# Decay rows of one half batch moved into matmuls of their own, and the first value loads moved forward in the load queue

## The chip, the cores and the metric

The kernel runs on one core of a Trainium2 chip. The metric is the device time of one execution in microseconds; 272.35 us is the median of five executions before the change (271.96 to 273.83). A separate execution was recorded by the profiler: it took 271.63 us, of which 269.7 us lie between its first and its last instruction (the span). All times inside the kernel are counted from the start of that span.

Engine names: PE is the matrix engine (PEld its weight loads), DVE the vector engine, ACT or ScalarE the activation engine, POOL the general engine, SP the engine that here only issues DMA transfers. SPq, ACTq and POOLq are their DMA-issuing queues.

## The reference

Eight batches of eight heads, 576 positions, head width 64, then a feed-forward block with a 3-tap convolution:

```python
scores = (q @ k.T) / sqrt(64) + cum[i] - cum[j]     # cum = cumsum(log(clip(f)))
attn   = softmax(where(j > i, -1e9, scores))
x      = (attn @ v), heads side by side              # 576 x 512 per batch
h      = relu(x @ w_in)                              # 576 x 1024
gate   = sigmoid(conv3(h, conv_w))                   # along the positions
out    = (h * gate) @ w_out                          # 576 x 512
```

All inputs and the output are fp32. The term `cum[i] - cum[j]` is called the decay.

## The kernel before, in words

**Tiling.** Work on attention is cut into 16 half batches `hb` of four heads, and each of these into two head pairs `i`. Scores are held transposed, keys on the partitions and queries along the row. For a pair there is one block of diagonal tiles (`diag_scores`, L326, eight 128x128 matmuls onto a causal mask that a matmul by the identity, L330, puts down first), and per head one block of the tiles off the diagonal (`off_scores`, L315, matmuls of 448, 64, 320 and 192 columns); the last 64 keys of all four heads form one tail block (`tail_scores`, L301). ScalarE takes each block to an fp16 tile by one exp (L338, L324, L310). `pv` (L340) multiplies these by the values `va`, whose 65th column is one, so that the softmax sum comes along; `norm` (L359) divides.

**Queries and keys.** `load_qk` (L106) loads q and k by transposing DMAs on SP. An fp32 number is transposed as two 16-bit halves, so of 128 partitions the odd ones hold the upper halves, which are used as bf16, and the even ones hold lower halves. `clamp` (L116) multiplies the even partitions by zero on DVE. Three even partitions then carry the decay: k's 96 and 98 hold the upper and lower bf16 part of minus `cum` over the scale, against ones in q; q's 126 holds the upper part against minus one in k. So a single matmul of full height gives q·k plus decay. There is a ring of four q tiles (`stq`) and four k tiles (`stk`).

Who puts the decay rows in differs. For half batch 0 `clamp` writes the constants, and ScalarE (first pair) and POOL (second pair) issue small row DMAs (`rows_first`, L122). For half batch 1, `clamp` stops at partition 96, POOL copies constant rows from the tile `consts` (`fill`, L129) and then three rows from `khi_sb` and `klo_sb` (`rows_of`, L139 to L143). From half batch 2 on the rows come by way of DRAM (`kd`). `fill_sources` (L542) writes `consts` by three memsets on DVE, early. From half batch `CLAMPS` (8) on, q's even partitions are cleared by a constant copy of 48 rows on POOL in place of DVE's clamp.

**Values.** `load_v` (L158) loads fp32 values by SP, five DMAs a half batch, into two buffers `vf`, one per batch in turn; `cast_v` (L167) brings them to fp16 on DVE. The first load is held until a one-element memset of DVE (L250), so that it is not issued ahead of that point. `HALVES` (16) says up to which half batch values are loaded by halves.

**MoE.** After both half batches of a batch, its attention output is transposed on PE (`xpose_pe`) and copied (`xpose_out`). Per 128 columns of d_ff: `moe1` (L420) on PE, `relu` (L430) on ScalarE into one of four `ht` tiles, two `conv` steps on DVE (L455, L457), `tanh` on ScalarE, `gate` (L469) on DVE, which frees the `ht` tile; `moe2` (L484) then multiplies by w_out, 128 positions at a time.

**What sets the order.** Instructions up to L269 stand in the order written. From L527 on the kernel keeps a list of tasks, each with the engines it may run on, an assumed duration, what it depends on, a key (a due time in units of head pairs) and the buffers that it takes and gives. `play` (L713) plays this list through before anything is built and hands out, engine by engine, the ready task with the lowest key; the result is a fixed order of instructions per engine. Each engine runs its own list strictly in order. `hold` (L149) is a one-element write that keeps a later weight load from being issued early; `WAITS` (L550) names the half batch and the side whose preparation releases each of the four loads of w_out.

**Queues.** SP issues one transfer after another. In the program as built a transfer issued by SP or ScalarE also waits for the end of the transfer issued eight before it on these two; POOL's have the same rule among themselves. SP's order before is: q and k of half batch 0 (four transfers), q1, k1, ten loads of batch 0's values, q2, k2, five loads of values, q3, k3, and so on.

Of the kernel before, what the change touches and what calls it, by code (L numbers as in the profile page):

```python
# [9 lines left out]
FP32 = mybir.dt.float32  # L10
# [8 lines left out]
def kernel(  # L19
# [11 lines left out]
    nc = tc.nc  # L31
# [103 lines left out]
    def rows_of(hb):  # L135

        tq, tk = stq_t[hb % RING], stk_t[hb % RING]
        c = slice(hb * HH, (hb + 1) * HH)
        if hb == 1:  # L139
            nc.gpsimd.dma_start(tk[96:97, 0:HS], khi_sb[c, :])  # L140
            nc.gpsimd.dma_start(tk[98:99, 0:HS], klo_sb[c, :])
            nc.gpsimd.dma_start(tq[126:127, 0:HS], khi_sb[c, :])
            return  # L143
        nc.gpsimd.dma_start(tq[126:127, 0:HS], kd[0:1, c, :].rearrange("j h s -> j (h s)"))
        row = HS + 64
        nc.gpsimd.dma_start(bass.AP(tensor=tk.tensor, offset=int(tk.offset) + 96 * row, ap=[[2 * row, 2], [1, HS]]),
                            kd[:, c, :].rearrange("j h s -> j (h s)"))

# [86 lines left out]
    load_qk(1, 0, 4)  # L235
    for side in range(2):
        clamp(0, side, 0, 2)
    rows_first(0, nc.scalar)

# [10 lines left out]
    nc.vector.memset(vf_t[0][0:1, 0, 0, 0:1], 0.0)  # L250
    load_v(0, 0, HH)
    load_v(0, HH, H)
# [14 lines left out]
    for t in range(NHT):  # L267
        nc.gpsimd.memset(ht_t[t][:, :, 0:HT_0], 0.0)
        nc.gpsimd.memset(ht_t[t][:, :, HT_0 + S:HT_W], 0.0)  # L269

# [25 lines left out]
    def scores(sc, hb, k0, q0, w, start=True, stop=True):  # L296

        nc.tensor.matmul(sc, stk_t[hb % RING][:, k0:k0 + 128], stq_t[hb % RING][:, q0:q0 + w],  # L298
                         start=start, stop=stop, skip_group_check=True)
# [242 lines left out]
    def fill_sources():  # L542
        z = consts.bitcast(FP32)
        nc.vector.memset(z, 0.0)
        nc.vector.memset(z[0:2, :], PAIR)
        nc.vector.memset(z[32:33, :], MINUS)

    CLAMPS, HALVES, LANDING = 8, 16, 3.0
    HELD, POOLED = 4, 4
    WAITS = ((3, 0), (3, 1), (4, 0), (4, 1))  # L550
# [8 lines left out]
    t_fsrc = task({"DVE": 3.1}, [], -9, fill_sources)  # L559
    for hb in range(NHB):  # L560
        key = 2 * hb - 5.5
        ring = [x for j in range(2) for x in t_qk[hb - RING, j]] if hb >= RING else []
        b = hb // 2
        even, landed = [], []
        for s in range(2):
            if hb == 1:
                x = task({"ACT": 0.01}, [], -9, lambda: None, lag=(0.3, 3.8)[s])
            elif hb:
                last = x = task({"SP": 3.0}, ring, key + 0.1 * s, lambda hb=hb, s=s: load_qk(hb, 0, 4, s),
                                lag=LANDING, dma=3.1, behind=last)  # L570
            if hb:
                landed.append(x)
            if hb:
# [5 lines left out]
            if hb and (s or hb < CLAMPS):  # L579
                even.append(task({"DVE": 0.9}, [x], (2 * hb - 3 if hb > 1 else -5) + 0.2 * s,  # L580
                                 lambda hb=hb, s=s: clamp(hb, s, 0, 4, 96)))
        t_half = None
        if b == 0 and hb < 2:
            t_half = task({"ACT": 0.01}, [], -9, lambda: None, lag=(6.5, 9.3)[hb])
            t_v[b] = t_half
        elif hb < HALVES:
            last = t_half = task({"SP": 3.2}, [t_cast[hb - 4, p] for p in range(2)] if b >= 2 else [], key + 0.2,
                                 lambda b=b, h=HH * (hb % 2): load_v(b, h, h + HH), lag=2.3, dma=3.0, behind=last)
        elif hb % 2 == 0:
            last = t_v[b] = task({"SP": 3.5}, [t_cast[2 * b - j, p] for j in (4, 3) for p in range(2)] if b >= 2 else [],  # L590
                                 key + 1.2, lambda b=b: load_v(b), lag=2.3, dma=6.0, behind=last)
# [4 lines left out]
        if hb:  # L596
            t_rows[hb] = even + [task({"POOL": 1.1 if hb > 1 else 1.6}, landed, 2 * hb - 3.6 if hb > 1 else -9 if hb > 1 else -1.0,
                                      lambda hb=hb: rows_of(hb), lag=LANDING + 1.0)]
        else:
            t_rows[hb] = []  # L600
        for p in range(2):
            t_cast[hb, p] = task({"DVE": 0.75 if p == 0 else 0.42},
                                 [t_half or t_v[b]] + ([t_pv[2 * hb - 5, 1]] if hb >= 3 else []), 2 * hb - 1.1 + 0.5 * p,
                                 lambda hb=hb, p=p: cast_v(hb, p, nc.vector), lag=0.2)

        for p in range(2):
# [10 lines left out]
            x = task({"PE": 0.9}, t_rows[hb], i + 0.1, lambda i=i: diag_scores(i), take="sc")  # L617
            t_qk[hb, p] = [t_tail, x]
            mask = task({"ACT": 1.02}, [x], i + 0.1, lambda i=i: diag_exp(i), take="pm", give=[("sc", x)])
            for s in range(2):  # L620
                x = task({"PE": 0.46}, t_rows[hb], i + 0.2 + 0.4 * s, lambda i=i, s=s: off_scores(i, s),
# [9 lines left out]
            t_norm[i] = task({"DVE": 1.05}, [t_pv[i, 1]], i - 0.0, lambda i=i: norm(i) if i else [norm(i), hold(w_in_f16)],  # L631
                             take="xn" if i % PPB == 0 else None, give=[("O", t_pv[i, 0])])
            if i == 0:
                t_win = task({"POOL": 1.0}, [t_norm[0]], -0.5, lambda: nc.gpsimd.dma_start(
                    w_in_f16, moe_w_in.rearrange("(cc p) ff -> p cc ff", p=128)), lag=2.0, dma=6.5)
        if hb % 2:
# [10 lines left out]
    start = [PPB * (b0 + nb) + 1.0 for b0, nb in GROUPS]  # L647
    start += [start[-1] + 4.0, start[-1] + 6.0]
    t_exp, t_late = [], []
    for g, (b0, nb) in enumerate(GROUPS):  # L650
# [3 lines left out]
        for ff in range(NFF):  # L654
            key = start[g] + 0.8 * (start[g + 1] - start[g]) * ff / NFF
            relus = []
            for t in range(nt):
# [5 lines left out]
                relus.append(task({"ACT": 0.18 + w / 1200.0}, [x] + relus[0:1], key + 0.05 * t - 1.5,  # L663
# [10 lines left out]
            t_gate[g, ff] = task({"DVE": 0.1 + n / 1800.0 if g == LAST else 0.2 + n / 1050.0}, [x], key - 1.5, lambda g=g, ff=ff: gate(g, ff),  # L674
# [36 lines left out]
    AHEAD, QUEUED = 3.0, 8.0  # L711

    def play():  # L713
        busy = {"PE": 11.5, "ACT": 12.0, "DVE": 12.0, "POOL": 14.0, "SP": 19.0}
        ready = {e: [] for e in busy}
        dma_free, clock = 21.5, 0.0
# [112 lines left out]
```

## Time and profile before

| | |
|---|---|
| median of five executions | 272.35 us (271.96 to 273.83) |
| profiled execution, its span | 271.63 us, 269.7 us |
| busy over the span: PE, DVE, ACT, POOL | 241.1, 226.5, 211.8, 58.9 us |
| mean granted PE clock | 0.981 |
| PE idle of 0 to 80 us; of 80 to 230 us | 20.0 us; 0.7 us |
| first score matmul of half batch 0, of half batch 1 | 11.4, 24.5 us |
| first moe1 matmul, first conv | 37.36, 40.02 us |
| transfers on SP's queue | 32.0 MB, 69.1% of 16 DMA engines' span |

Busy time is a sum over one engine's instructions; 89% for PE is a mean over a beginning in which it waits and a long stretch in which it never does. In rows of stretches the columns are: stretch, its length, busy us and count for each engine, granted PE clock (1.00 is full speed), mean busy share of the DMA engines, GB/s. In rows of the timeline: start, duration, engine, line, operation, output and input, count, and in brackets how long the engine had been idle and what ended that. In rows of waits: who waited for whom, us in total, how often, the longest.

### The profile page before, as it was taken

The numbers are of one execution on the slowest core, as the hardware profiler recorded it, in microseconds if no ns is written. First come the engines' busy times: TensorE is split into PE (matmuls) and PEld (weight loads), VectorE is DVE, ScalarE is ACT, GpSimd is POOL, SyncE is SP. The second block draws the span as 40 slices with busy tenths as digits, with TensorE's granted clock in tenths as the row PEclk, the third lists the DMA queues.
The fourth block names the chain that finished last, engine by engine and source line by source line (L and its number), as shares of the span: only waits on it lengthen the run. The fifth ranks groups of instructions, "written<-read, shape, count | busy, mean of one in ns | idle before, by whom it ended". The sixth has DMA issues, their size and how long they took to land.

```text
span 269.7 us, 6621 instructions
## 1 busy us (share of the span) xinstructions
PE 241.1 (89%) x2602; PEld 165.1 (61%) x2602; DVE 226.5 (84%) x401; ACT 211.8 (79%) x347; POOL 58.9 (22%) x124
## 2 busy tenths in 40 slices
PE   2955779877999999999999999999999999989990
PEld 1334557655777677676776677667776767554640
DVE  5963539999799999999989989999899999978751
ACT  5171829889879999989988898989999998577552
POOL 4491110631221240332415050404110100000000
PEclk9997979999999999999999999999999999999997
DMA  7999999999999999999999999999410201022015
GB/s 140 224 195 185 220 179 211 192 233 195 199 204 200 210 244 187 220 223 239 258 200 178 216 268 192 190 119 252 128 48 32 80 0 71 10 117 80 0 48 226
DMA packets 121284, 44.58 MB, mean 165 GB/s; under 512 B 115560, under 2 KB 116596, under 8 KB 121254
## 3 DMA queue, kind: packets, MB, share of 16 engines
q1 hardware_dynamic: 115088, 32.00, 69.1%
q0 software_dynamic: 5840, 12.01, 16.7%
q8 instruction: 20, 0.33, 0.5%
q10 hardware_dynamic: 326, 0.17, 0.3%
q14 instruction: 10, 0.08, 0.1%
HBM read 13.99 MB, written 9.58 MB: 87 GB/s over the span
## 4 chain that ended last, share of the span: by engine, by line
PE 62%; DMA 9%; DVE 7%; SPq 7%; issue 6%; ACT 6%; POOL 0%; ACTq 0%; DVEq 0%; POOLq 0%
PE mm L425 18%; PE mm L487 18%; PE sc L298 10%; PE O L356 7%; DMA stk<-in_k_dram 6%; SPq L110 5%; PE sc L330 4%; DMA vf<-in_v_dram 2%; PE sc L500 2%; SPq L163 2%; DVE u L457 2%; DVE u L455 2%; PE mm L393 2%; ACT ht L438 1%; DMA out_dram<-ob 1%
## 5 line engine op out<-in xcount | busy, mean ns | idle before, releaser
L425 PE MATMUL mm<-xt,w_in_f 128*128 128x288 f16 x512 | 79.9, 290 | 1.7 <-DVE xt L413 0.4
L298 PE MATMUL sc<-stq,stk 128*128 128x128 bf16 (+3 forms) x576 | 67.1, 242 | 7.4 <-ACT pm L338 3.6
L324 ACT ACTIVATE po<-sc 128x1024 f16<-128x1024 f32 x64 | 64.5, 1028 | 2.0 <-PE sc L298 1.5
L438 ACT ACTIVATE ht<-mm 128x288 f16<-128x288 f32 x128 | 52.0, 414 | 11.7 <-PE mm L425 10.7
L298 PEld LDWEIGHTS <-stk 128*128 128x128 bf16 x576 | 42.4, 99 | 28.4 <-issue 8.5
L425 PEld LDWEIGHTS <-w_in_f 128*128 128x128 f16 x512 | 47.7, 99 | 18.6 <-issue 3.4
L487 PE MATMUL mm<-w_out_f,hg 128*128 128x512 f16 x248 | 58.4, 379 | 0.7 <-ACT xt L411 0.6
L455 DVE SCALAR_TENSOR_TENSOR u<-ht,cwt 128x576 f32<-128x576 f16 x64 | 51.5, 812 | 5.4 <-ACT ht L438 4.7
L457 DVE SCALAR_TENSOR_TENSOR u<-ht,cwt,u 128x576 f32<-128x576 f16 x64 | 51.5, 811 | 0.5
L475 DVE SCALAR_TENSOR_TENSOR hg<-hg,ht 128x576 f16<-128x576 f16 x56 | 41.7, 752 | 3.8 <-ACT hg L467 3.5
L467 ACT ACTIVATE hg<-u,cwt 128x576 f16<-128x576 f32 x56 | 43.4, 779 | 1.0 <-DVE u L457 0.9
L338 ACT ACTIVATE pm<-sc 128x1024 f16<-128x1024 f32 x32 | 32.9, 1027 | 12.0 <-PE sc L298 11.9
L487 PEld LDWEIGHTS <-hg 128*128 128x128 f16 x248 | 23.5, 98 | 24.3 <-issue 0.9
L356 PE MATMUL O<-va,po 128*128 128x65 f16 x640 | 36.5, 194 | 1.2 <-ACT po L324 1.0
L356 PE MATMUL O<-va,pm 128*128 128x65 f16 x256 | 31.1, 194 | 3.0 <-DVE xn L369 1.8
L356 PEld LDWEIGHTS <-po 128*128 128x128 f16 x640 | 30.5, 97 | 2.4 <-ACT po L324 1.8
L132 POOL DMA_DIRECT2D stq<-consts x23 | 12.6, 549 | 75.3 <-PE sc L298 34.2
L356 PEld LDWEIGHTS <-pm 128*128 128x128 f16 x256 | 24.1, 98 | 5.7 <-DVE xn L369 2.7
L369 DVE TENSOR_TENSOR xn<-O,rc 128x640 f16<-128x640 f32 x32 | 26.4, 825 | 1.1
L330 PE MATMUL sc<-trib,identb 128*128 128x512 bf16 x64 | 24.7, 387 | 1.5 <-ACT po L324 1.4
L511 ACT ACTIVATE ob<-mm 128x512 f32<-128x512 f32 x23 | 13.7, 597 | 11.1 <-PE mm L487 10.7
L522 POOL DMA_DIRECT2D out_dram<-ob x10 | 7.5, 748 | 40.1 <-ACT ob L511 20.7
(112 smaller groups left out, 222.5 us busy)
## 6 DMA issues: line engine op xcount, KB each, us to landing
vf<-in_v_dram SPq DMA_DIRECT2D x64, 128.0 KB, 3.9
out_dram<-ob POOLq DMA_DIRECT2D x10, 512.0 KB, 5.2
out_dram<-ob SPq DMA_DIRECT2D x10, 256.0 KB, 2.1
stq<-consts POOLq DMA_DIRECT2D x8, 216.0 KB, 4.6
vf<-in_v_dram SPq DMA_DIRECT2D x16, 64.0 KB, 5.2
w_in_f<-in_moe_w_in_dram POOLq DMA_DIRECT2D x1, 1024.0 KB, 10.4
w_out_f<-in_moe_w_out_dram POOLq DMA_DIRECT2D x4, 256.0 KB, 5.7
out_dram<-ob SPq DMA_DIRECT2D x2, 512.0 KB, 2.8
```

Of the source, the lines that this page charges most:

```text
L298: nc.tensor.matmul(sc, stk_t[hb % RING][:, k0:k0 + 128], stq_t[hb % RING][:, q0:q0 + w], start=start, stop=stop, skip_group_check=True)
L324: nc.scalar.activation(p_of[i, s][:, 0:1024], sc_of.pop((i, s)), AF.Exp, scale=SCALE)
L330: nc.tensor.matmul(sc[:, 512 * s:512 * (s + 1)], identb, trib, start=True, stop=False, skip_group_check=True)
L338: nc.scalar.activation(p_of[i, 2], sc_of.pop((i, 2)), AF.Exp, scale=SCALE)
L356: nc.tensor.matmul(O[:, s, 65 * Q:65 * (Q + 1)], w, va[:, h, m, :], start=(m == 0), stop=(m == Q))
L425: nc.tensor.matmul(ps[:, 0:w], w_in_f16[:, cc, 128 * ff:128 * (ff + 1)], xt[:, cc, w * t:w * (t + 1)], start=(cc == 0), stop=(cc == NCC - 1))
L438: nc.scalar.activation(ht[:, 0, HT_0 + w * t:HT_0 + w * (t + 1)], ps[:, 0:w], AF.Relu)
L455: nc.vector.scalar_tensor_tensor(u, hl, cwt[:, ff, 0:1], hc, op0=ALU.mult, op1=ALU.add)
L457: nc.vector.scalar_tensor_tensor(u, hr, cwt[:, ff, 1:2], u, op0=ALU.mult, op1=ALU.add)
L467: nc.scalar.activation(hv, u, AF.Tanh, scale=cwt[:, ff, 2:3])
L475: nc.vector.scalar_tensor_tensor(hv, hv, 1.0, hc, op0=ALU.add, op1=ALU.mult)
L487: nc.tensor.matmul(ps, chunk(g, ff, c), w_out_f16[:, ff, :], start=(ff == 0), stop=(ff == NFF - 1))
```

## The change

The diff does eight things, in the order of the program.

1. SP's order at the start: q1, first half of batch 0's values, k1, second half of the values. What holds the first values is no longer a memset on DVE but a one-element activation on ScalarE, behind its issue of the first pair's decay rows.
2. ScalarE writes two tiles, `dk` and `dq`, inside the values buffer of batch 1 (`vf_t[1]`, not yet in use): `dk` is zero but for minus ones in its first three rows, `dq` is one everywhere. POOL then copies the upper and lower parts of half batch 1's decay into `dk`'s rows 0 and 1 and the upper part into `dq`'s row 2 (`load_decay`), right after the rows of half batch 0's second pair.
3. For half batch 1 each score matmul is followed by a second one, `dk` by `dq`, onto the same output: 36 more matmuls. Its q and k are clamped over all 128 partitions, and its constant fills and its `rows_of` go.
4. The loads of batch 1's values wait for the scores of half batch 1, since they overwrite `dk` and `dq`.
5. `consts` is written after the norm of pair 1, as three tasks.
6. `warm`: two matmuls of 512 columns into an unused buffer, five times, with the lowest urgency, after the second pair of half batch 0.
7. `CLAMPS` 8 to 6, `HALVES` 16 to 8, `WAITS` later for the first load of w_out.
8. Keys and assumed costs of the planner: norm, clamp, cast, relu, gate, the start of each MoE group, and how many us of transfers may be queued.

```diff
-        if hb == 1:
-            nc.gpsimd.dma_start(tk[96:97, 0:HS], khi_sb[c, :])
-            nc.gpsimd.dma_start(tk[98:99, 0:HS], klo_sb[c, :])
-            nc.gpsimd.dma_start(tq[126:127, 0:HS], khi_sb[c, :])
-            return
...
+    def decay_tiles(hb, dk, dq):
+        dec_of[hb] = dk, dq
+        for t, x in ((dk, 0.0), (dk[0:3], MINUS), (dq, PAIR)):
+            z = t.bitcast(FP32)
+            nc.scalar.activation(z, one1[0:z.shape[0]].broadcast_to(z.shape), AF.Copy, bias=x, scale=0.0)
+
+    def load_decay(hb):
+        (dk, dq), c = dec_of[hb], slice(HH * hb, HH * (hb + 1))
+        nc.gpsimd.dma_start(dk[0:1, 0:HS], khi_sb[c, :])
+        nc.gpsimd.dma_start(dk[1:2, 0:HS], klo_sb[c, :])
+        nc.gpsimd.dma_start(dq[2:3, 0:HS], khi_sb[c, :])
...
-    load_qk(1, 0, 4)
+    load_qk(1, 0, 4, 0)
     for side in range(2):
         clamp(0, side, 0, 2)
     rows_first(0, nc.scalar)
+    nc.scalar.mul(vf_t[0][0:1, 0, 0, 0:1], one1[0:1, 0:1], 0.0)
+    load_v(0, 0, HH)
+    load_qk(1, 0, 4, 1)
+    load_v(0, HH, H)
+    early = vf_t[1].rearrange("p h k d -> p (h k d)")
+    decay_tiles(1, early[:, 0:HS // 2 + 32].bitcast(BF16), early[:, HS // 2 + 32:HS + 32].bitcast(BF16))
...
     rows_first(1, nc.gpsimd)
-    nc.vector.memset(vf_t[0][0:1, 0, 0, 0:1], 0.0)
-    load_v(0, 0, HH)
-    load_v(0, HH, H)
+    load_decay(1)
...
+    def warm():
+        ps = mm_pool.tile([128, 512], FP32, name="mm")
+        for t in range(2):
+            nc.tensor.matmul(ps, identb, trib, start=True, stop=True)
...
-                         start=start, stop=stop, skip_group_check=True)
+                         start=start, stop=stop and hb not in dec_of, skip_group_check=True)
+        if hb in dec_of:
+            dk, dq = dec_of[hb]
+            nc.tensor.matmul(sc, dk[:, k0:k0 + 128], dq[:, q0:q0 + w],
+                             start=False, stop=stop, skip_group_check=True)
...
-    CLAMPS, HALVES, LANDING = 8, 16, 3.0
+    CLAMPS, HALVES, LANDING = 6, 8, 3.0
-    WAITS = ((3, 0), (3, 1), (4, 0), (4, 1))
+    WAITS = ((3, 1), (3, 1), (4, 0), (4, 1))
+    WARM = {0: 5}
...
-    t_fsrc = task({"DVE": 3.1}, [], -9, fill_sources)
+        if hb == 2:
+            t_fsrc = None
+            for z in ((0, 96, 0.0), (0, 2, PAIR), (32, 33, MINUS)):
+                t_fsrc = task({"DVE": 1.03}, [t_norm[1], t_fsrc], 3.0, lambda z=z: fill_source(*z))
...
-            last = t_half = task({"SP": 3.2}, [t_cast[hb - 4, p] for p in range(2)] if b >= 2 else [], key + 0.2,
+            last = t_half = task({"SP": 3.2}, [t_cast[hb - 4, p] for p in range(2)] if b >= 2 else
+                                 t_qk[1, 0] + t_qk[1, 1], key + 0.2,
...
-            t_norm[i] = task({"DVE": 1.05}, [t_pv[i, 1]], i - 0.0, lambda i=i: norm(i) if i else [norm(i), hold(w_in_f16)],
+            t_norm[i] = task({"DVE": 1.05}, [t_pv[i, 1]], i - 0.5, lambda i=i: norm(i) if i else [norm(i), hold(w_in_f16)],
...
+        if hb in WARM:
+            x = None
+            for _ in range(WARM[hb]):
+                x = task({"PE": 0.44}, [t_pv[2 * hb + 1, 1], x], 999, warm, take="mm", lag=0.05)
...
-    start = [PPB * (b0 + nb) + 1.0 for b0, nb in GROUPS]
-    start += [start[-1] + 4.0, start[-1] + 6.0]
+    start = [PPB * (b0 + nb) + x for (b0, nb), x in zip(GROUPS, (1.0, 1.0, 1.5, 2.0, 1.5, 1.0, 1.0, 1.0))]
+    start += [PPB * B + 5.0, PPB * B + 7.0]
...
-                relus.append(task({"ACT": 0.18 + w / 1200.0}, [x] + relus[0:1], key + 0.05 * t - 1.5,
+                relus.append(task({"ACT": 0.18 + w / 1200.0}, [x] + relus[0:1], key + 0.05 * t - 2.0,
...
-            t_gate[g, ff] = task({"DVE": 0.1 + n / 1800.0 if g == LAST else 0.2 + n / 1050.0}, [x], key - 1.5, ...
+            t_gate[g, ff] = task({"DVE": 0.1 + n / 1800.0 if g == LAST else 0.2 + n / 1050.0}, [x], key - 0.0, ...
...
-    AHEAD, QUEUED = 3.0, 8.0
+    AHEAD, QUEUED = 3.0, 10.0
```

## The prediction

> **What bounds the kernel now.** I read the busy times of stretches first, since a share over the whole span mixes stages. The columns are the stretch, PE, PEld, DVE, ACT and POOL busy (with counts), granted PE clock, DMA share, GB/s:
>
> ```profile
> 20.00:25.00 5.00, 1.74 (x36) 1.46 (x37) 1.79 (x6) 0.09 (x1) 0.84 (x2) 0.87 1.20 169
> 25.00:30.00 5.00, 4.68 (x42) 3.29 (x41) 1.54 (x3) 3.35 (x5) 1.01 (x2) 0.79 1.16 216
> 35.00:40.00 5.00, 3.26 (x20) 2.08 (x21) 1.56 (x4) 1.83 (x3) 0.97 (x2) 0.74 1.23 166
> 45.00:50.00 5.00, 4.66 (x67) 3.52 (x64) 4.97 (x10) 5.00 (x9) 2.17 (x3) 1.00 1.33 172
> 65.00:70.00 5.00, 3.96 (x58) 2.95 (x55) 4.97 (x8) 4.16 (x6) 1.31 (x2) 1.00 1.16 217
> 100.00:120.00 20.00, 19.98 (x228) 14.37 (x226) 18.84 (x31) 18.29 (x34) 3.52 (x8) 1.00 1.18 217
> ```
>
> Three regimes: until 40 us nobody is full (everything waits for arrivals), from 45 to 70 DVE is (4.97 of 5), from 80 PE is (19.98 of 20). So a microsecond is won or lost in two ways only: by when the first MoE block hands DVE its long queue of work (40.02), and by PE work or PE gaps after about 70. What holds the first MoE block back is read from the timeline and the waits of 20 to 35 us:
>
> ```profile
> 12.57 7.04 SPq L163 DMA_DIRECT2D vf<-in_v_dram  x10
> 18.00 0.43 DVE L170 TENSOR_SCALAR va<-vf 128x512 f16<-128x512 f32 x1 [1.27 <-DMA vf<-in_v_dram]
> 18.11 0.97 POOL L140 DMA_DIRECT2D stk<-khi_sb  x1
> 19.55 0.50 POOL L142 DMA_DIRECT2D stq<-khi_sb  x1
> 24.50 0.37 PE L298 MATMUL sc<-stq,stk 128*128 128x64 bf16 x4 [2.48 <-DMA stq<-khi_sb]
> 37.36 4.94 PE L425 MATMUL mm<-xt,w_in_f 128*128 128x288 f16 x24 [0.38 <-DVE xt L413]
> 40.02 0.82 DVE L455 SCALAR_TENSOR_TENSOR u<-ht,cwt 128x576 f32<-128x576 f16 x1 [2.71 <-ACT ht L438]
> ```
>
> ```profile
> POOL stk L146 <- DMA stk<-in_k_dram: 5.4, 1, 5.4
> DVE va L170 <- DMA vf<-in_v_dram: 3.2, 1, 3.2
> PE sc L298 <- DMA stq<-khi_sb: 2.5, 1, 2.5
> ```
>
> Half batch 1's keys were down at 15.83 and clamped by 16.73, but its scores start at 24.50: its three decay rows are issued by POOL only at 18.11 to 20.05 (behind the set-up memsets and two constant fills) and land 4.9 to 5.6 us after issue. Half batch 0 in turn waits for its values until 18.00. And both PE droughts end at half clock:
>
> ```profile
> 24.00:25.00 1.00, 0.50 (x5) 0.42 (x6) 1.00 (x4) 0.09 (x1) 0.00 (x0) 0.50 1.28 290
> 38.00:39.00 1.00, 1.00 (x5) 0.60 (x4) 0.00 (x0) 0.41 (x1) 0.00 (x0) 0.50 1.00 227
> ```
>
> **Step 1, start of half batch 1's scores (24.50 now).** SP's order becomes q1, v0a (five issues), k1, v0b, q2, k2. ScalarE's release of the values is its third row issue (ends 8.36) plus one element, about 8.6, before SP is free at 9.85: no wait. q1 is issued unchanged, lands at 7.41+4.6 = 12.0. The fifth v0a issue waits for the transfer eight issues before it, now q1, so about 12.1; k1 is issued at about 12.7 instead of 9.90 and, with its 5.9 us to landing, is down at 18.6 (2.8 later). v0a, issued 9.9 to 12.7 behind q1, lands at about 15.5 (2.5 earlier). v0b goes out at 15.4 to 18.4, q2 at about 18.5 instead of 19.65.
> Decay: ScalarE's three fills are 1184, 1184 and 1152 fp32 long; nearest row is the 64x576 fp32 activation of 0.68 us and the 128x1024 one of 1.02, so 1.15 to 1.35 each, 3.5 to 4.1 together, from 8.6 to 12.1 or 12.7. I take 12.2. ScalarE was idle there (5.89 us before the first exp at 12.22), so cost 0 to 0.5, taken 0; the exp is next in its queue and PE's second score slot waits for it. Behind the fills POOL issues the three rows at 12.3 to 14.0 and, at 5 to 5.6 us, they land by 19.5. The two dram copies of the rows and POOL's memsets come 1.7 us later; nobody needs them before half batch 2.
> DVE: casts of v0a at 15.5 to 16.7, clamp of q1 (0.9), norm of pair 0 and the one-element release of w_in, then clamp k1. Pair 0's PV still waits for the tail exp (ends 16.40, unchanged), and PE has the second diagonal block first, so it ends at 18.5; norm to 19.7; clamp k1 to 20.6. PE finishes pair 1's PV at 20.7. Hence scores start at about 20.8: minus 3.7. End cases: k1 as slow as v0a was from its first issue (5.4 us behind more data), 22.4; everything kinder, 20.3.
>
> **Step 2, length of half batch 1.** 36 added matmuls. A head pair's scores in the trace stand 0.11 us apart per four of 64 columns, 0.22 per four of 128 and about 0.45 per head of 448+64+320+192. So 0.12 + 4x0.22 + 4x0.45 = 2.8 us at full clock, 5.6 at half. The Trainium skill ("TensorE: Matmul & The Clock Gate", Back-to-back issue gap) speaks against the cheap figure: in real streams of weight load and matmul it puts 128 columns at about 81 ns, where this trace has 55 (0.22/4); by the page the 20 narrow ones cost about 0.6 more, 3.4 in all. I use the trace. The page's remark that a weight load costs by columns and not by rows fits: three useful rows are paid as 128.
> Ten warm matmuls of 512 columns: 0.22 each at full clock by the pairs of L330, 2.2 us; four stand after the last PV, where PE waits for DVE's norm and its transposed copy, so 0.9 is covered; the other 1.3 is on PE between blocks.
> PE's list from the first score to the last PV is then tail 0.5, two diagonals of 1.33, four off-diagonals of 0.9, four PV of 0.5, transposes 0.5, conv weights 0.65, warm 1.3: about 11.2 us, nearly gapless because ScalarE needs only 6.4. Before, it was 10.1 (24.50 to 34.6) with gaps. So the last PV is at 32.0, its norm at 33.2, transposes at 33.3 instead of 36.36 (where DVE, in order, also sat on the clamp of k2 until 35.3; that clamp now stands behind the first conv).
> The 3.06 us of constant memsets move from 11.34-15.0 to after pair 1's norm, into DVE idle of 1.96+1.79+3.2 us (20 to 31); they lengthen the wait of the v0b casts to about 24, ahead of the first PV that needs them at 25.
>
> **Step 3, first MoE block.** moe1 moves from 37.36 to about 34.3. With PE kept busy its clock should stay 1.00 where it was 0.50 at 38 to 40; the first two tiles then take 0.49 each instead of 0.96, so the first conv comes 2.1 instead of 2.66 us after: about 36.5, against 40.02: minus 3.5. The skill's rule (same page, Why this matters for your kernels) is that only PE gaps above about 3 us drop the clock; here 22.02 to 24.50 already did, a gap of 2.5. By the rule step 3's clock term would be nothing and the sum minus 3.0; the row decides.
>
> **Step 4, does the stream of loads follow?** Bytes on SP are the same. Two constant fills (67.5 and 63 KB) vanish at half batch 1 and the dip to 78 GB/s at 17-18 us, where SP was waiting, goes, so k2 lands at 32 to 34.4 (34.41 now). New: the first load of batch 1's values waits for PE's last decay matmul and ScalarE's fills; behind it in SP's queue stand q3, k3 and everything later. That last score is at about 30.2; SP came to this issue at 31.33 because k2's issue took 7.58. Cover 1.1 us; beyond it, every microsecond delays q3 and k3 by one. Half batch 3's rows also no longer queue behind POOL's w_out issue, which held POOL 5.5 us (to 47.77): worth something to PE's gaps of 4.9 us between 40 and 70, taken as 0 since DVE is full there.
>
> **Step 5, later edits.** Clamps of q for half batches 6 and 7 (2x0.87 us of DVE) become 48-row fills by POOL (216 KB, 4.6 us to land): beside PE at 99.5%, 0. Values from half batch 8 in one go: 20 fewer SP issues, SP is ahead by then: 0. New keys for relu, norm, gate and MoE start: PE lost only 0.7 us of the 150 us from 80 to 230, so they can hardly win there; taken 0, bounds -0.7 to +4. The last 30 us keep nearly the same order.
>
> **Sum.** -3.5 from the first conv (the start brings 3.7, longer PE takes back, norm and clock give back), +0.1 for the exp. 271.63 for the profiled execution becomes 268.2; the median of 272.35 lies 0.7 above that execution, so 268.95: I say 269.0.
>
> **Rivals.**
> A, slower: the new keys loosen the PE-bound stretch. gate, which frees one of four ht buffers and feeds moe2, loses 1.5 of urgency while relu gains 0.5. For: DVE is at 94% and ACT at 91% there, so little is spare. Against: PE has scores, moe1 and moe2 to choose from, and DVE loses 1.74 us. It decides against the change once PE's share from 80 to 230 falls below 96.3% (4.9 us = 3.4 + 1.4); at 96% it gives about 274.5.
> B, no change: the gain is hidden. DVE starts MoE 3.5 early but its 19 us of batch 0 (8 blocks of 0.81+0.81+0.75) runs out before half batch 3's attention is through, as its loads are still paced by DMA. For: k2 and k3 landed at 34.4 and 43.2. Against: half batch 3's rows were late by POOL, not by k3. About 271.8.
> C, larger: half batch 3's rows come 5 us sooner and PE's gaps in the DVE-full stretch shrink by 2 to 3: about 266.3.
> That decay rows still end last (landing after 22.4) is the weak end of the main case: 270.6.
>
> **Numbers.** Main case 0.59, own range 267.3 to 270.8; C 0.12; B 0.14; A 0.15. A measurement of this kernel tells 0.5%, 1.36 us, from no change. Faster 0.59+0.12 less a sliver = 0.70; same 0.15; slower 0.15. Range 266.2 to 272.9 leaves out most of A and the tip of C.
>
> **What would show it.** Right: first score of half batch 1 near 20.8, waiting for DVE or its own PV, not for a row; first conv near 36.5; clock 1.00 from 24 to 41; DVE full from about 41; PE full from 80 on with under 1 us of gaps. Wrong: a wait of SP for PE ahead of batch 1's values; the first exp after 12.7; PE below 97% after 80; k1 landing after 20.

## The result and the profile after

The changed kernel takes 0.9923 of the time before, with a 95% interval of 0.9898 to 0.9947. On the 272.71 us of before measured beside it that is 270.6 us: 2.1 us less (1.4 to 2.8). The forecast was 269.0 us, 3.35 less. So the sign was right and the range held the time, but the gain is some 60% of what was forecast. Measured again beside the experiments, the same kernel gives 0.9921 [0.9897, 0.9944]. The ratios compare the executions within 1.5% of the fastest of the same kernel: of the kernel before these are 38 of 39, of the kernel after only 10 of 20, and its median over all twenty is 272.55 us, hardly below that of before (beside the experiments 13 of 15 count, and the medians over all are 270.11 and 272.11); of the versions below only the keys alone, the old urgencies and the one without warm matmuls have a profile of such an execution, and from the other profiles I read the order and the starts of things, not totals.

The profiled execution of the kernel after took 271.4 us with a span of 269.1 (before: 271.63 and 269.7). The busy times of the stretches that the prediction showed, now of the kernel after:

```profile
20.00:25.00 5.00, 4.33 (x75) 3.65 (x76) 4.36 (x10) 2.81 (x4) 0.79 (x1) 1.00 1.31 185
25.00:30.00 5.00, 5.00 (x75) 3.91 (x74) 3.09 (x6) 3.46 (x4) 1.02 (x2) 1.00 1.11 205
35.00:40.00 5.00, 4.42 (x37) 2.91 (x35) 2.28 (x5) 3.05 (x6) 1.03 (x2) 1.00 1.25 236
45.00:50.00 5.00, 2.92 (x23) 1.91 (x23) 5.00 (x12) 3.43 (x6) 0.92 (x1) 0.99 1.15 154
65.00:70.00 5.00, 4.64 (x56) 3.16 (x53) 4.97 (x10) 4.01 (x7) 2.02 (x4) 1.00 1.08 237
100.00:120.00 20.00, 18.86 (x230) 13.95 (x228) 17.18 (x30) 17.26 (x31) 6.75 (x12) 1.00 1.13 219
```

PE's drought of 20 to 25 us is gone (1.74 us busy became 4.33), and the clock there is 1.00 instead of 0.87. But between 45 and 50 us PE now works 2.92 us where it worked 4.66, while DVE is full. The beginning gained, and the next stretch gave some of it back. The timeline of the kernel after, at the places that the prediction named:

```profile
8.48 3.44 ACT L152 ACTIVATE vf<-one 128x1184 f32<-128x1184 f32 x3
10.09 2.97 SPq L174 DMA_DIRECT2D vf<-in_v_dram  x5
12.22 0.54 POOL L156 DMA_DIRECT2D vf<-khi_sb  x1
12.45 1.02 ACT L364 ACTIVATE pm<-sc 128x1024 f16<-128x1024 f32 x1 [0.53 <-PE sc L320]
13.10 3.08 SPq L110 DMA_TRANSPOSE stk<-in_k_dram  x1
16.29 0.43 DVE L181 TENSOR_SCALAR va<-vf 128x512 f16<-128x512 f32 x1 [5.17 <-DMA vf<-in_v_dram]
21.74 0.19 PE L320 MATMUL sc<-stq,stk 128*128 128x64 bf16 x1
36.37 3.69 PE L451 MATMUL mm<-xt,w_in_f 128*128 128x288 f16 x24 [0.38 <-DVE xt L439]
38.33 0.82 DVE L481 SCALAR_TENSOR_TENSOR u<-ht,cwt 128x576 f32<-128x576 f16 x1 [2.01 <-ACT ht L464]
```

Half batch 1's first score comes at 21.74 instead of 24.50 and waits for no decay row: no bracket stands behind it. (L324, which reads `vf`, is the added decay matmul; `vf<-khi_sb` is a decay row on its way into `dk` or `dq`.) ScalarE's fills took 3.44 us and the first exp moved by 0.23. Of the 2.8 us won at 21.74, moe1 keeps 1.0 (36.37 instead of 37.36) and the first conv 1.7 (38.33 instead of 40.02). What lies between is read from DVE's list in the same timeline:

```profile
29.39 0.18 DVE L299 COPY cw<-mm 128x24 f32<-128x24 f32 x1 [1.36 <-PE mm L297]
...
30.72 0.87 DVE L119 TENSOR_SCALAR stq<-stq,lim 96x2304 uint16<-96x2304 uint16 x1
...
31.51 0.21 DVE L393 RECIPROCAL rc<-O 128x10 f32<-128x10 f32 x1
...
32.64 0.20 PE L382 MATMUL O<-va,pm 128*128 128x65 f16 x1 [1.40 <-DVE xn L395]
```

The last PV of pair 2 had ended at 29.94. Its norm starts only at 31.51, since DVE, strictly in order, first waited for PE's transposes of the conv weights, then did eight small operations on them, then the clamp of half batch 2's q. PE's next PV waits 1.40 us for that norm. In the second profile of the kernel after, the one taken beside the experiments, the same place is worse, because the q that the clamp needs lands late:

```profile
32.46 0.88 DVE L119 TENSOR_SCALAR stq<-stq,lim 96x2304 uint16<-96x2304 uint16 x1 [2.06 <-DMA stq<-in_q_dram]
...
34.38 0.20 PE L382 MATMUL O<-va,pm 128*128 128x65 f16 x1 [3.57 <-DVE xn L395]
```

**An account of PE.** From rows of one microsecond each (clock times busy time is work at full clock, the remainder of the busy time is lost to the clock, the remainder of the row is idle) the span of a run is the sum of three parts. Some records of matmuls can be missing, so single figures are good to about a microsecond. "Again" is the second profile of the kernel after, "no warm" the version below without the warm matmuls; cells are work / idle / lost, in us.

| | before | after | again | no warm |
|---|---|---|---|---|
| 0 to 40 | 22.6 / 14.9 / 2.5 | 28.5 / 9.8 / 1.7 | 26.8 / 13.2 / 0 | 25.6 / 11.6 / 2.8 |
| 40 to 70 | 24.5 / 5.1 / 0.4 | 22.5 / 5.8 / 1.7 | 25.4 / 4.6 / 0 | 25.1 / 4.8 / 0.2 |
| 70 to end | 191.0 / 8.7 / 0 | 190.8 / 8.3 / 0 | 189.7 / 7.3 / 0 | 188.7 / 7.6 / 0 |
| sum | 238.2 / 28.6 / 2.9 | 241.8 / 23.9 / 3.3 | 241.9 / 25.1 / 0 | 239.4 / 23.9 / 3.0 |
| span | 269.7 | 269.1 | 267.0 | 266.3 |

The change takes 4.7 and 3.6 us of idle time from PE in the two profiles of after, in the first all of it before 40 us, in the second less than half, and adds 3.7 of work. At 40 us PE is 5.9 and 4.2 us of work ahead, at 50 us only 3.1 and 1.9 (work from 40 to 50 is 6.5 and 6.9 us against 9.3). That is no more than the added work. At 70 us the leads, less the added work, are 0.2 and 1.3 us, and the remainder comes behind it. The third part moves as much as the others: the clock takes 2.9 us before, 3.3 in the first profile of after (from 16 to 19 and from 50 to 53 us) and nothing in the second. In the second, idle time won and work added nearly cancel, and the 2.7 us of shorter span are about what the clock took before. The account is a sum that must come out; it says where time lies, not why.

### The profile page after: what moved, and what is told of

The parts are those of the page before. It is cut to its first block, busy times and chain, and to the rows that moved or that the text cites. A ratio compares the mean times of both kernels' runs of the same rounds, so it can differ in the third digit from the quotient of the medians.

```text
span 269.1 us, 6679 instructions
## 1 busy us (share of the span) xinstructions
PE 245.2 (91%) x2648; PEld 169.0 (63%) x2648; DVE 224.8 (84%) x400; ACT 214.8 (80%) x349; POOL 59.4 (22%) x124
## 4 chain that ended last, share of the span: by engine, by line
PE 68%; DVE 11%; DMA 9%; ACT 5%; SPq 3%; issue 2%; POOL 0%; DVEq 0%; ACTq 0%
PE mm L451 19%; PE mm L513 18%; PE sc L320 12%; PE O L382 9%; DMA vf<-in_v_dram 6%; PE sc L356 4%; DVE u L483 2%; PE sc L526 2%; PE mm L419 2%; SPq L174 2%; DVE xn L395 2%; DMA stk<-in_k_dram 1%; DVE hg L501 1%; DMA stk<-klo 1%; ACT ht L464 1%
## 5 line engine op out<-in xcount | busy, mean ns | idle before, releaser
L320 PE MATMUL sc<-stq,stk 128*128 128x128 bf16 (+3 forms) x576 | 70.2, 244 | 5.1 <-ACT pm L364 2.6
L320 PEld LDWEIGHTS <-stk 128*128 128x128 bf16 x576 | 43.5, 99 | 25.0 <-issue 7.1
L451 PEld LDWEIGHTS <-w_in_f 128*128 128x128 f16 x512 | 47.1, 98 | 18.0 <-issue 3.7
L382 PE MATMUL O<-va,po 128*128 128x65 f16 x640 | 37.9, 197 | 0.1
L382 PE MATMUL O<-va,pm 128*128 128x65 f16 x256 | 32.0, 197 | 4.6 <-DVE xn L395 3.8
L382 PEld LDWEIGHTS <-po 128*128 128x128 f16 x640 | 31.7, 99 | 1.3 <-ACT po L350 0.4
L382 PEld LDWEIGHTS <-pm 128*128 128x128 f16 x256 | 25.0, 100 | 7.5 <-DVE xn L395 4.7
L537 ACT ACTIVATE ob<-mm 128x512 f32<-128x512 f32 x24 | 14.3, 597 | 11.0 <-PE mm L513 10.7
```

What stands on the lines that cost most here:

```text
L382: nc.tensor.matmul(O[:, s, 65 * Q:65 * (Q + 1)], w, va[:, h, m, :], start=(m == 0), stop=(m == Q))
L451: nc.tensor.matmul(ps[:, 0:w], w_in_f16[:, cc, 128 * ff:128 * (ff + 1)], xt[:, cc, w * t:w * (t + 1)], start=(cc == 0), stop=(cc == NCC - 1))
```

## The experiments

All ratios are to the kernel before, measured on the same chip beside each version. Nothing of the computation is changed except where the expectation says so.

**The later edits alone, and the new structure alone.** In one version the kernel before gets only the planner's constants and keys of the change, in the other the kernel after gets those of before back. The diff is of the latter; it goes on with the keys of clamp, cast, norm, relu, gate and the starts of the groups, and the former is the reverse, applied to the kernel before.

```diff
-    CLAMPS, HALVES, LANDING = 6, 8, 3.0
+    CLAMPS, HALVES, LANDING = 8, 16, 3.0
-    WAITS = ((3, 1), (3, 1), (4, 0), (4, 1))
+    WAITS = ((3, 0), (3, 1), (4, 0), (4, 1))
-    AHEAD, QUEUED = 3.0, 10.0
+    AHEAD, QUEUED = 3.0, 8.0
...
```

> The kernel before with only the later edits (keys, starts of the MoE groups, CLAMPS 6, HALVES 8, WAITS, QUEUED): no decay tiles, loads in the old order. Theory 1 (later edits are worth nothing, as step 5 had it): 0.998 to 1.003, first conv at 40.0. Rival A (the new keys cost): 1.004 to 1.015, with attention of half batch 2 later on ScalarE than in the kernel before (its tail exp after 44). Rival C (they gain in the stretch where DVE is full): 0.990 to 0.997.

> The changed kernel with the old keys, starts, CLAMPS, HALVES, WAITS and QUEUED: decay tiles, load order and warm matmuls alone. Theory 1 (all of the gain is in the opening): 0.990 to 0.995, as the whole change. If the new keys cost (rival A): better than the whole change, 0.986 to 0.990. If half of the gain is the keys': 0.995 to 1.0.

Measured: keys alone 1.0149 [1.0107, 1.0191]; structure alone 1.0413 [1.0381, 1.0445]. Both together, which is the kernel after, ran in the same comparison:

> The changed kernel once more, unaltered, as the mark for the runs beside it and for a second trace. Theory 1 (the shorter opening of half batch 1 is what is gained, 1.7 us at the first conv): again 0.990 to 0.995 of the kernel before. Rival (the gain is chance of one profiled execution): within 0.3% of 1. In the trace: half batch 1's first score near 21.7, first conv near 38.3, PE clock below 1 somewhere between 45 and 56 us.

It gave 0.9921 [0.9897, 0.9944]. So the parts do not add: plus 4.1 us and plus 11.2 us by themselves (1.49% and 4.13% of 272.1), minus 2.1 together. The keys alone lie at the upper end of what rival A gave, the structure alone outside all that was expected. Two details of the expectation for the kernel after missed: in its second profile the first conv came at 40.06, not near 38.3, and the clock stayed at 1.00 from 45 to 56 us. Of the structure with the old keys, the waits between 100 and 180 us, where the kernel before hardly lets PE stand:

```profile
DVE stk L119 <- DMA stk<-in_k_dram: 11.4, 2, 7.4
ACT hg L493 <- DVE u L483: 10.1, 6, 4.1
```

```profile
120.00:180.00 60.00, 50.80 (x522) 34.09 (x521) 43.47 (x73) 43.35 (x72) 13.96 (x24) 0.94 1.20 185
```

DVE waits up to 7.4 us for one k that lands late, ScalarE up to 4.1 us for DVE, and PE is busy 50.80 of 60 us (this profile is of an execution of 289.83 us, the median of the version is 283.21, so the lengths are large for it). Neither place is touched by the structural edit, and the kernel after, with the same structure and other keys, keeps PE busy for all of those 60 us; so I put the waits down to the order that `play` works out from the new durations and the old keys.

Which of the constants matter with the new structure was tried in two steps. First the old urgencies with the new constants of the loads (the constants in the diff above stay as in the kernel after):

> The kernel after with its own constants for the loads (clamps by fills from half batch 6 on, values in one piece from half batch 8 on, the wait of the w_out loads, the depth of the load queue in the planner), but with the old urgencies of clamp, cast, norm, relu, gate and the old starts of the MoE blocks. Nothing is left out. The version with all of these old was 1.041. If the loads made that loss (k issued late behind ring buffers at 132 and 161 us): 0.990 to 1.005, and no wait for k over 3 us from 120 to 175. If the urgencies of DVE and ScalarE made it (ScalarE's wait for DVE at tanh, 14 us): 1.025 to 1.045, the waits for k still there.

Measured 1.016 [1.0114, 1.0207], between the two expectations: set back in this order, the constants of the loads account for about half of the way from 1.041 to 0.992, the urgencies for the other half. Second, only the three keys that rival A named set back:

```diff
-    start = [PPB * (b0 + nb) + x for (b0, nb), x in zip(GROUPS, (1.0, 1.0, 1.5, 2.0, 1.5, 1.0, 1.0, 1.0))]
-    start += [PPB * B + 5.0, PPB * B + 7.0]
+    start = [PPB * (b0 + nb) + 1.0 for b0, nb in GROUPS]
+    start += [start[-1] + 4.0, start[-1] + 6.0]
-                relus.append(task({"ACT": 0.18 + w / 1200.0}, [x] + relus[0:1], key + 0.05 * t - 2.0,
+                relus.append(task({"ACT": 0.18 + w / 1200.0}, [x] + relus[0:1], key + 0.05 * t - 1.5,
...
-            t_gate[g, ff] = task({"DVE": 0.1 + n / 1800.0 if g == LAST else 0.2 + n / 1050.0}, [x], key - 0.0, lambda g=g, ff=ff: gate(g, ff),
+            t_gate[g, ff] = task({"DVE": 0.1 + n / 1800.0 if g == LAST else 0.2 + n / 1050.0}, [x], key - 1.5, lambda g=g, ff=ff: gate(g, ff),
```

> The kernel after with the three keys that rival A named set back to their values of before: the start of the MoE blocks, relu (0.5 less urgent) and gate (1.5 more urgent); all other new constants and the new structure stay. Nothing is left out. Rival A, turned round (the new keys loosen the stretch where PE is full): 0.985 to 0.990 and PE's idle time of 80 to 230 stays under 1. If the new keys are what makes the new structure run, as the versions with old keys (1.041 and, with the new load constants, 1.016) suggest: 1.010 to 1.020, with idle time of PE over 4 between 60 and 230. If the rest of the keys (clamp, cast, norm) carries it: 0.990 to 0.996.

Measured 1.0104 [1.0064, 1.0144]. A row of its stretches (same columns as above):

```profile
120.00:180.00 60.00, 55.32 (x616) 38.91 (x613) 49.74 (x84) 48.08 (x83) 15.45 (x29) 0.97 1.21 214
```

PE, full there in the kernel after (60.00 of 60), is busy 55.32 (in an execution of 280.39 us; the median of the version is 276.54). Rival A had the size right for the new keys with the old structure (1.0149), not the place (PE is busy 99.3% of 80 to 230 us there), and the sign wrong with the new structure: with it, it is the old ones, the more urgent gate among them, that go with gaps in the full stretch. Which of the three keys does it was not tried. The version is 4.9 us slower than the kernel after (1.0104 less 0.9923, times 272.4), though its profile has the first conv at 37.12, 1.2 us earlier.

**Without the warm matmuls.** The body of `warm` is left out, the order is kept.

```diff
     def warm():
-        ps = mm_pool.tile([128, 512], FP32, name="mm")
-        for t in range(2):
-            nc.tensor.matmul(ps, identb, trib, start=True, stop=True)
+        return
```

> The changed kernel in the same order, with its ten warm matmuls left out. Theory 1 (they keep the clock up through the gaps at 31 to 36 us): the granted clock falls to 0.5 at the first MoE tiles near 36 to 39 us, first conv 0.5 to 0.8 later, time 0.2 to 0.4% longer than the whole change. Rival (they only occupy PE): last PV of half batch 1 up to 1.3 us earlier, first conv 0.4 to 1 earlier, clock unchanged, time 0.2 to 0.4% shorter.

Measured 0.9906 [0.9875, 0.9937], not to be told from the kernel after. The stretch of 35 to 40 us:

```profile
35.00:40.00 5.00, 4.76 (x21) 2.90 (x21) 2.31 (x4) 2.23 (x5) 1.03 (x2) 0.50 1.17 224
```

The clock is at 0.50 there, as it was in the kernel before from 38 to 40 us, and at 1.00 in both profiles with the warm matmuls. So they do hold the clock, as the first theory said, but what they win by it is no more than they cost: the 2.8 us that the clock takes stand against 2.5 us less work, and from the first score to the first conv it is 16.74 us here and 16.59 in the kernel after. Nor is the gain of the whole change the clock's alone: over the executions compared the mean granted clock is 0.982 here, 0.980 before and 0.990 in the kernel after beside them, and the time is no longer than that of the kernel after.

**The price of the added matmuls.** Each of the 36 is issued twice.

```diff
-            nc.tensor.matmul(sc, dk[:, k0:k0 + 128], dq[:, q0:q0 + w],
-                             start=False, stop=stop, skip_group_check=True)
+            for last in (False, True):
+                nc.tensor.matmul(sc, dk[:, k0:k0 + 128], dq[:, q0:q0 + w],
+                                 start=False, stop=stop and last, skip_group_check=True)
```

> The kernel after, in the same order, with each of the 36 added matmuls of half batch 1 issued twice, so that its decay is counted double there (the computation is changed in that one part). Measures step 2's 2.8 us by itself. If PE's work between the first score and the last PV of half batch 1 is on the path one for one (prediction's step 2): first conv 2.5 to 3 us later, ratio 0.9925 plus 2.8/272.1, 1.001 to 1.004. If the added matmuls fall into PE's idle time (2.6 to 4.4 us from 20 to 40, 3.1 to 3.5 from 40 to 50): at most 1 us, 0.992 to 0.996. At the page's 81 ns for 128 columns instead of 55 the step would be 3.4: 1.004 to 1.006.

Measured 1.0017 [0.9986, 1.0048]: 2.6 us above the kernel after (0.0094 of 272.4; about 1.1 to either side). From the same first score, 21.74, the first conv comes at 40.63 instead of 38.33, 2.3 later. That is the one-for-one case. In the timeline of the kernel after the pairs of 128 columns stand like this:

```profile
22.41 0.22 PE L320 MATMUL sc<-stq,stk 128*128 128x128 bf16 x1
22.47 0.22 PE L324 MATMUL sc<-vf 128*128 128x128 bf16 x1
22.53 0.22 PE L320 MATMUL sc<-stq,stk 128*128 128x128 bf16 x1
22.58 0.22 PE L324 MATMUL sc<-vf 128*128 128x128 bf16 x1
```

They are 0.056 us apart at a granted clock of 1.00: the prediction's row prices them, not the 81 ns that the Trainium skill gives ("TensorE: Matmul & The Clock Gate", Back-to-back issue gap).

**The rows back in the tiles, in the order of the kernel after.** This undoes the decay tiles alone, with the planned order fixed; SP's new first loads stay. Three row writes by POOL, issued once, behind the clamp of half batch 1's k, take the tiles' place.

```diff
-    decay_tiles(1, early[:, 0:HS // 2 + 32].bitcast(BF16), early[:, HS // 2 + 32:HS + 32].bitcast(BF16))
...
-    load_decay(1)
+    def rows_late():
+        tq, tk, c = stq_t[1], stk_t[1], slice(HH, 2 * HH)
+        nc.gpsimd.dma_start(tk[96:97, 0:HS], khi_sb[c, :])
+        nc.gpsimd.dma_start(tk[98:99, 0:HS], klo_sb[c, :])
+        nc.gpsimd.dma_start(tq[126:127, 0:HS], khi_sb[c, :])
...
```

> The kernel after, in the same order, but with half batch 1's decay as rows of its q and k tiles again: all 128 partitions clamped, then three rows written once by POOL's DMAs behind the clamp of k, ahead of the issue of w_in; no fills by ScalarE, no 36 added matmuls, and batch 1's values wait for nothing. Nothing is left out. The rows are issued near 20.5 to 22 and land 4.2 to 4.8 later, so the first score comes near 26.5 instead of 21.2 to 21.7. If the gain is the early start (prediction's step 1, less step 2's 2.8): first conv 2.2 to 3 later than in the kernel after, ratio 1.000 to 1.004. If the gain is made by the written-out order and the planner's keys, and the early start is spent again between 40 and 70: ratio 0.989 to 0.995, with PE's idle time of 20 to 40 larger by 4 to 5, that of 40 to 70 smaller, and PE's work smaller by 1.5 to 2.8.

Measured 1.0019 [0.9975, 1.0063]: 2.6 us above the kernel after (0.0096 of 272.4; about 1.4 to either side). Its timeline:

```profile
20.08 0.55 POOL L258 DMA_DIRECT2D stk<-khi_sb  x1 [3.65 <-DVE stk L119]
...
24.57 0.37 PE L323 MATMUL sc<-stq,stk 128*128 128x64 bf16 x4 [4.29 <-DMA stq<-khi_sb]
...
41.37 0.82 DVE L484 SCALAR_TENSOR_TENSOR u<-ht,cwt 128x576 f32<-128x576 f16 x1 [2.01 <-ACT ht L467]
```

The first score waits 4.29 us for a row again, at almost the time of the kernel before (24.50), and the first conv is 3.0 later than in the kernel after. So in this order the separate decay tiles are worth about 2.6 us, their own matmuls paid. (The clock is part of it: with the rows back PE ran at 0.51 from 25 to 30 us, with the tiles at 1.00.) This and the kernel before differ by nothing that can be told (1.0019, interval across 1), although the order of everything behind is the new one: with the rows, the new order and the moved loads are worth nothing that shows, and the measured gain is that of the decay tiles in this order. An earlier form of this version wrote the three rows again behind every clamp, which is another computation; its 1.140 says nothing of the question.

**Less waiting on DVE.** The conv weights stand behind the norm of pair 3 and the clamp of half batch 2's q behind the norm of pair 2, by moving two entries of the played order.

```diff
     order, est = play()
+    behind_of(t_cw, t_norm[3])
+    behind_of(t_clamp_q2, t_norm[2])
```

> The kernel after, with its written-out order kept except for two moves: the transposes of the conv weights and DVE's eight small operations on them stand behind the norm of pair 3, and the clamp of half batch 2's q behind the norm of pair 2. Nothing is left out. Theory of the queue: the norm of pair 2 (31.51 in the kernel after, though its last PV ended at 29.95) is late because DVE works in order behind the wait for the conv weights; then it now starts near 30.2, PE's wait of 1.40 us for it goes, the last PV of half batch 1 ends about 1.4 earlier (32.6), the first conv is 1 to 1.5 us earlier, and the ratio to the kernel before is 0.986 to 0.989. Rival, the account of PE (the end is PE's work plus its idle time plus what the clock loses, and an idle microsecond taken from 20 to 40 us turns up between 40 and 70, where DVE is the slower engine): the wait goes, the idle time of 20 to 40 falls by about 1.4, that of 40 to 70 grows by as much, ratio 0.990 to 0.994 as the kernel after.

Measured 0.9939 [0.9912, 0.9967]. DVE's rows of its timeline:

```profile
30.83 0.22 DVE L393 RECIPROCAL rc<-O 128x10 f32<-128x10 f32 x1 [1.25 <-PE O L382]
...
38.28 0.82 DVE L481 SCALAR_TENSOR_TENSOR u<-ht,cwt 128x576 f32<-128x576 f16 x1 [1.99 <-ACT ht L464]
```

The norm of pair 2 now waits for PE and no longer for DVE's own queue. This execution had its first score of half batch 1 at 23.29, 1.55 later than the profile of after, and yet the same first conv; so the path from one to the other became 1.6 us shorter, as the queue theory said. (It is 14.99 us here, 16.59 in the profile of after, and 16.58 in three versions with the same DVE list here: the old urgencies, the three keys, the values not moved. Only in the second profile of after, where q came late, is it longer, 18.75.) The time did not follow: 0.9939 lies at or above the kernel after, and 0.986 to 0.989 is outside the interval. The rival's forecast holds for the time: what is won at this place does not show at the end. That the idle time turns up at one particular later place I do not take from this profile.

**Less waiting on ScalarE between 40 and 50.** On top of the version without warm matmuls, the tanh of the third MoE block is moved behind the masked exp of pair 4, which it held up.

```diff
     order, est = play()
+    behind_of(tanh_2, mask_4)
```

> The kernel after without the ten warm matmuls (0.991 by itself), in the same order, with one move on ScalarE: the tanh of the third MoE block, which waits for DVE until 46.93 and holds the masked exp of pair 4 behind it to 47.61, stands behind that exp. Nothing of the result is left out. If ScalarE's wait in order is what makes PE idle between 40 and 50 (3.1 us): the exp starts near 45.5, PE's idle time of 40 to 50 falls to 1 to 2, ratio 0.984 to 0.989. If that idle time is given back later, since DVE is the slower engine until 70: 0.989 to 0.993, idle time of 50 to 70 larger by what 40 to 50 lost.

Measured 0.9934 [0.9892, 0.9976].

```profile
44.95 1.02 ACT L363 ACTIVATE pm<-sc 128x1024 f16<-128x1024 f32 x1
46.63 0.78 ACT L492 ACTIVATE hg<-u,cwt 128x576 f16<-128x576 f32 x1 [0.66 <-DVE u L482]
```

The exp starts 2.7 us earlier (44.95 instead of 47.61), but PE's idle time from 40 to 50 falls only from 3.1 to 2.7 us (7.32 busy of 10), and no gain is seen: 0.984 to 0.989 lies outside the interval. ScalarE's order was not what starves PE there; DVE, busy 10.00 of those 10 us, is the candidate that is left, argued and not shown.

**The values not moved forward.** SP's first order set back, all else kept.

```diff
+    load_qk(1, 0, 4, 1)
     load_v(0, 0, HH)
-    load_qk(1, 0, 4, 1)
     load_v(0, HH, H)
```

> The kernel after, in the same order, but with SP's first loads as before: q and k of half batch 1, then the values of half batches 0 and 1. The decay tiles and all else stay. Nothing is left out. In the kernel after the first values are cast at 16.29 instead of 18.00. Set back, k of half batch 1 lands about 2.8 earlier and the values about 1.7 to 2.5 later; the first PV is late by as much, and the first score of half batch 1, which stands behind the PV of pairs 0 and 1, comes near 22.8 to 23.5. By the sum of the prediction (all of the start is worth its time): ratio 0.996 to 1.000. By the account of PE with the time given back between 40 and 70: 0.990 to 0.995.

Measured 0.9887 [0.9802, 0.9972], from two executions only: too wide to place it among the others. In its trace the values are cast at 17.76 (16.29 in the kernel after), and the first score of half batch 1 comes at 23.81. In nine profiles with the values moved forward these dates are 15.38 to 16.86 and 20.54 to 23.29. So the forward move does bring the start, by 2 us against the profile of after; whether the end sees it stays open. Only the upper part of what the prediction's sum would give (0.996 to 1.000) is excluded.

No version tried is shown to beat the kernel after; those with a lower ratio (without warm matmuls, and the one just told) have intervals that cover it.

## Why the prediction was right, and where it was not

**Step 1, the start.** Right in kind: the first score waits for its predecessors on PE and for no row, the fills took 3.44 us (3.5 to 4.1 forecast), the exp was late by 0.23, k1 went out at 13.10 and landed near 19.3. (In the second profile the exp came at 12.76, late by 0.54, of which 0.3 is the whole start.) The score is 2.8 earlier in one profile, 3.2 in the other (21.31), against 3.7. Such dates differ by the execution, and the forecast of 20.8 lies inside the 20.54 to 23.29 of the nine profiles. In the two profiles of after the missing part is the landing of the values: cast at 16.29 and 16.86 instead of 15.5, and with it the norm of pair 0 and the clamp of k1.

**Step 2, the length of half batch 1.** The price of the matmuls was right: 2.8 forecast, 2.6 by doubling them, with the spacing that the trace gave. That they lie on the path was right too. What the list lacked is DVE's queue: it has no wait of PE for the norm of pair 2, which DVE, behind the conv weights and a clamp, could start only at 31.51. From the first score to the end of the last PV it was 12.4 us instead of 11.2, and that end came at 34.2 instead of 32.0. In the second profile, with the late q at the head of DVE's list, it is worse again.

**Step 3, the first MoE block, failed.** Two things are wrong in it. The first conv is 1.7 and not 3.5 us earlier. And the sum took the microseconds of the first conv as those of the end. The second profile of the kernel after speaks against it:

```profile
40.06 0.82 DVE L481 SCALAR_TENSOR_TENSOR u<-ht,cwt 128x576 f32<-128x576 f16 x1 [2.01 <-ACT ht L464]
```

Its first conv is at 40.06, as late as before (40.02), and PE had waited 3.57 us on the way, yet its span is 267.0, 2.7 us shorter than before and 2.1 shorter than in the profile with the conv at 38.33. The version with a shorter DVE queue has the path to the conv shortened by 1.6 us and gains nothing. On the other side, the two versions that delay the conv by 2.3 and 3.0 us (the matmuls twice, the rows back) lose 2.6 us each, nearly all of the delay. So a delay came through and an advance did not; why, the runs leave open. One reading behind the step was too sharp: in the prediction's own row of 45 to 50 us DVE is not the only full engine, ScalarE is busy 5.00 and PE 4.66 of 5. The clock term was real in the trace (0.50 without the warm matmuls, 1.00 with), and in time it paid no more than the warm matmuls cost.

**Step 4, the loads.** SP hardly waited for PE ahead of batch 1's values, but the forecast cover of 1.1 us was gone: SP's issue of k2 ended at 30.63, the last decay matmul at 30.81, and the first half of the values went out at 30.89 (31.33 before). And k2, forecast down at 32 to 34.4, landed at about 35.2, and q2 is what DVE waits for in the second profile. The stream of loads did not come forward by what the start won, which is what rival B put forward.

**Step 5, the later edits, failed in its working.** It took the new keys as 0 with bounds of minus 0.7 to plus 4, by themselves. By themselves they cost 4.1 us, and the structure without them 11.2. That the net of the order is near nothing (1.0019 with the rows in the new order) is what is left of large terms that the prediction never formed; its zero was right by luck. Neither the profile of before nor the diff shows such terms; the played order of each combination would have had to be read.

**The rivals.** A: right in size for the keys alone, wrong in sign with the new structure; PE stayed at 99.2% of 80 to 230 us, well over the 96.3% from which it would have decided. B: its effect is there in part: PE is short of work from 40 to 50 us while DVE is full, and the lead over before at 70 us, less the added work, is 0.2 to 1.3 us. C: half batch 3's first row was issued 7 us sooner (41.22 instead of 48.49), but idle time from 40 to 70 shrank by 0.5 at most, not by 2 to 3.

**The sum.** Minus 3.35 was forecast, minus 2.1 measured. In the order of the kernel after, the decay tiles bring 2.6 us net; the rest of the change together, by the same version, costs 0.5 with an interval from minus 0.7 to plus 1.7. How the missing 1.2 us divide between the start, which won 0.5 to 0.9 less than forecast, and what is lost between 40 and 70 us, the runs do not settle. The values moved forward, the other half of the change's name, are not shown to gain by themselves. So the cause named is the right one, the early scores less their added matmuls; that the range held although the first conv came only half as much earlier and the later edits were large terms that cancel is in part luck.

## What to carry to other kernels

When a planner turns costs and keys into a fixed order, its constants and a structural edit cannot be priced apart: build both halves of the change; here each one by itself was worse than nothing. An earlier start of one stage need not be worth its time at the end; follow one engine's work, idle time and clock from the start to the end instead of the date of one event, and take more than one profile, since the same program put one event 1.7 us apart in two executions. In a list that an engine works through in order, look for what stands ahead of the instruction whose time you quote, small set-up work above all.

## What the runs showed that was not expected

The clock fell without a long gap. In the profile of after PE ran at 0.50 from 16 to 19 us, though its idle times in the five microseconds before were each under 0.7 us (it was busy 0.41, 0.85, 0.47, 0.43 and 0.59 of the five). The second profile of the same program stayed at 1.00 there with PE no busier before (0.10, 1.00, 0.33, 0.68 and 0.29). The row of 16 to 17 us, first of one, then of the other:

```profile
16.00:17.00 1.00, 1.00 (x10) 0.72 (x9) 0.71 (x2) 0.07 (x1) 0.87 (x6) 0.50 1.37 281
16.00:17.00 1.00, 0.90 (x11) 0.53 (x8) 0.14 (x1) 0.45 (x2) 0.82 (x7) 1.00 0.67 126
```

And it did not fall in a long one: in the second profile PE stood for 3.57 us before 34.38 (the line shown above), and the clock was 1.00 in every microsecond from 30 to 40. In the kernel before a wait of 2.48 us had ended at 0.50. A rule by the length of gaps does not tell these cases apart.
